# Value products in whole blocks of 128 queries, and an output projection of even units on 64x128 tiles

## The chip, the core and the metric

The kernel is one program on one core of a Trainium2 chip. Its engines work side by side, each in its own order, and wait for each other through semaphores: TensorE (PE in the profile, its weight loads PEld), VectorE (DVE), ScalarE (ACT), GpSimd (POOL) and SyncE (SP), which issues DMAs. The metric is the device time of one execution in microseconds (us). Lower is better.

## The reference

Attention over 8 batches and 8 heads of 576 positions with 64 dimensions, in which only scores within tau of their row's maximum count, then a mixture of 8 experts with one expert for each token:

```python
scores = scale * np.matmul(q, k.transpose(0, 1, 3, 2))
thresh = np.max(scores, axis=-1, keepdims=True) - tau
scores = np.where(scores >= thresh, scores, -1000000000.0)
attn = np.exp(scores - np.max(scores, axis=-1, keepdims=True))
x = np.matmul(attn / (np.sum(attn, axis=-1, keepdims=True) + 1e-09), v)   # tokens x 512, heads side by side
e_idx = np.argmax(x @ w_gate, axis=1)
...
out[mask] = gate_w[mask, None] * eom[mask, e, None] * (np.maximum(x[mask] @ w1[e], 0.0) @ w2[e])
```

All inputs and outputs are fp32.

## The kernel before

The attention treats a **unit** at a time: two batches (a = 0, 1) of one head, 32 units in all. The loop in `run` counts g through 16 **rounds** of nine **steps** (0 to 8). A round treats two units, an even one in steps 0 to 3 and an odd one in steps 5 to 8; step 4 (`ENDS`) takes the last 64 queries of both. In each step a string of letters (`USUAL`, `ROWS` and others) sets the order in which each engine receives its work; there is no scheduler.

- S, `scores` (L158 in step 4, L161 otherwise): 128 queries of both batches against 576 keys into PSUM. VectorE scales them and takes the row's extreme (L167), one instruction for each of two score tiles.
- e and f, `exp` (L177): ScalarE's exponentials of the two tiles. In the step after, VectorE masks and sums them (L189), with a threshold that GpSimd makes (L172).
- T, `remainder` (L222) and B, `blocks` (L264): TensorE transposes what was masked two steps earlier. o and c are ScalarE's copies of these out of PSUM: L247 (in step 4's turn four small ones, L237) and L279, into `PTa` (the first 256 queries) and `PTb` (the rest). L237's four copies take partitions 0-63, 64-127, 64-127, 0-63.
- V, `av_units` (L299): the value products. The weights are 64 columns of V for one batch and 128 keys (`vm[:, k, a]`, a 128x64 tile), or 64 keys at the end (64x64), and the transposed probabilities are read past them. An even unit's products stand in steps 5, 7 and 8 of its round, an odd unit's in steps 1, 2 and 3 of the next (`AV`). The sums stay in two PSUM banks (`self.banks`, named pab). X, `done`, copies them to SBUF (`X`, L303 and L305).
- R, `x_rows` (L341): the output projection. The stationary operand is a piece of `X`, 64 rows by 64 queries, the moving one `wx`: 80 columns, an identity of 64 and the 16 router weights. Even units have it in step 0, odd ones in step 4, between S and T. r, `x_copy` (L354), copies the result out of the same banks to `xl`; then GpSimd multiplies by the inverse sums (`x_out`, L363) and adds the logits.

In steps 0 and 4 the order is `ROWS = "SRTerofBc"`. On ScalarE this gives e, r, o, f, c. The value products of the following step write the banks that r and o read, and wait for o. R has its own place in PSUM at the very end alone.

In `X`, the 64-query block b of batch a lies on partitions of half a ^ (b % 2). Products of batch a and block parity o go to bank o and to half a ^ o. In steps other than 4, S, T and B use tiles of 64 rows by 128 columns, in step 4 S uses 64x64; R uses 64x64 in both places.

After the attention (about 450 us) the experts run on TensorE (L1184 to L1279) with the tokens that the router has sorted.

Of the kernel before, what the change touches and what calls it, by code (L numbers as in the profile page):

```python
# [8 lines left out]
F32 = mybir.dt.float32  # L9
# [7 lines left out]
P = 128  # L17
# [7 lines left out]
class Attention:  # L25
# [20 lines left out]
    def __init__(self, ctx, tc, ident, qkv, tau, wg, shape, router):  # L46
        self.tc, self.nc = tc, tc.nc
        nc = self.nc
        self.qkv = qkv
        self.B, self.H, self.S, self.D = shape  # L50
        self.NB = self.S // P
        self.M = self.NB * P
        self.R = self.S - self.M
        self.HS = self.S // 2
        self.KH = self.HS + self.R
        self.QK = 2 * self.S + 2 * self.KH
        self.QA = 2 * P
        self.NK = 2 * self.NB + 1
        self.nu = self.B // 2 * self.H
        self.router = router  # L60
        pool = lambda name, bufs, **kw: ctx.enter_context(tc.tile_pool(name=name, bufs=bufs, **kw))
        self.ld = pool("ald", self.LB)
        self.sp = pool("asp", 3)
        self.const = pool("aconst", 1)
        self.vld = pool("avld", self.VB)
        self.w2 = pool("aw2", 1)
        self.w3 = pool("aw3", 3)
        self.xp = pool("axp", 1)
        self.ps_s = pool("ps_s", 2, space=PSUM)
        self.ps_t = pool("ps_t", 1, space=PSUM)  # L70
        ab = pool("ps_ab", 1, space=PSUM)
        self.both = ab.tile([P, 1024], F32, name="pab").rearrange("p (a n) -> p a n", a=2)
        self.banks = [self.both[:, a] for a in range(2)]
        c = self.const
        self.ident = ident
        self.tau = c.tile([P, 1], F32, name="tau_sb")
        self.tau_in, self.wg_in = tau, wg
        warm = c.tile([P, 1], F32, name="warm")
        nc.vector.memset(warm, 0.0)
        nc.scalar.activation(warm, warm, AF.Exp)  # L80
        E2 = wg.shape[2]
        self.XW = self.D + E2
        self.wx = c.tile([P, self.H, self.XW], F32, name="wx")
        self.X = [c.tile([P, self.S], F32, name=f"X{i}") for i in range(2)]
        self.half = [slice(0, 64), slice(64, P)]
        for pp in self.half:
            nc.gpsimd.tensor_copy(
                self.wx[pp, :, 0 : self.D], ident[pp, None, pp].broadcast_to([self.D, self.H, self.D])
            )
        self.loaded, self.sums, self.rinv, self.LX = {}, {}, {}, None  # L90
        self.PTa, self.PTb, self.slot, self.live = {}, {}, 0, False
# [191 lines left out]
    def av_units(self, u):  # L283
        nc, NB, hs, D = self.nc, self.NB, self.half, self.D
        v = self.loaded[u][1]
        vm = v[:, 0 : NB * P].rearrange("p (k a d) -> p k a d", a=2, d=D)
        X = self.X[u % 2]

        def products(PT, half, k, start):
            PT = PT.rearrange("p k (b j) -> p k b j", j=D)  # L290
            nb, c0 = PT.shape[2], half * P
            for a, o in ((0, 0), (1, 0), (1, 1), (0, 1)) if k < NB else ((0, 0), (1, 1), (1, 0), (0, 1)):
                n = (nb - o + 1) // 2 * D
                out = self.banks[o][hs[a ^ o], c0 : c0 + n].rearrange("p (b j) -> p b j", j=D)
                if k < NB:
                    w, x, end = vm[:, k, a], PT[:, 4 * a + k, o::2], half and k == NB - 1
                else:
                    w, x, end = v[hs[a], NB * P :], PT[hs[a], self.NK - 1, o::2], not half
                nc.tensor.matmul(out, w, x, start=start, stop=bool(end), skip_group_check=True)  # L299

        def done(q0, c0, n):
            x = X[:, q0 : q0 + 2 * P].rearrange("p (b o j) -> p o b j", o=2, j=D)
            nc.scalar.copy(x, self.both[:, :, c0 : c0 + P].rearrange("p o (b j) -> p o b j", j=D))  # L303
            if n > 2 * P:
                nc.scalar.copy(X[:, q0 + 2 * P : q0 + n], self.banks[0][:, c0 + P : c0 + n - P])  # L305

        PT = self.PTa.pop(u)
        self.slot, self.live = 0, True
# [29 lines left out]

    def x_rows(self, u, ps):
        X, pp, W, h, NB = self.X[u % 2], self.half, self.XW, u % self.H, self.NB  # L340
        mm = lambda out, c0, k: self.nc.tensor.matmul(  # L341
            out, X[pp[k], c0 : c0 + 64], self.wx[pp[k], h], start=True, stop=True
        )
        for j in range(NB):
            for a in range(2):
                for c in range(2):
                    mm(ps[a][pp[c], j * W : (j + 1) * W], j * P + 64 * c, a ^ c)
        for a in range(2):
            mm(ps[0][pp[a], NB * W : (NB + 1) * W], self.M, a)

    def x_copy(self, xl, ps):
        for a, b in enumerate(ps):
            n = self.NB + 1 - a
            self.nc.scalar.copy(xl[:, a::2], b[:, 0 : n * self.XW].rearrange("p (j w) -> p j w", w=self.XW))  # L354

    def x_out(self, u, xl):
        nc, r, D, rt = self.nc, self.rinv[u], self.D, self.router
# [1143 lines left out]
```

## Time and profile before

| | |
|---|---|
| time, median of 3 runs | 874.05 us (871.35 to 875.64) |
| profiled execution | 871.86 us, its span 870.1 us |
| TensorE busy | 855.7 us, 98% of the span |
| VectorE busy | 716.7 us, 82% |
| ScalarE busy | 592.3 us, 68% |
| GpSimd busy | 442.6 us, 51% |
| granted TensorE clock, mean | 0.997 |

The shares are averages over two stages. In the slices of the page TensorE, VectorE and ScalarE stand at 9 tenths through the first half; in the second TensorE alone does. A busy TensorE is modelled: its rows overlap, and an end is later than the moment at which the next one can begin. Its pace is read from starts. A row of the timeline joins instructions that follow each other and are alike; every product in fp32 leaves two rows in the trace. A bracket gives the idle time ahead and what ended it.

### The profile page before, as it was taken

Reading aid. Unit: us, or ns where it says so; the run is one execution under the profiler, and the core shown is the slowest. Engines: PE = TensorE matmul, PEld = TensorE weight load, DVE = VectorE, ACT = ScalarE, POOL = GpSimd, SP = SyncE. Lnnn points to the kernel's source line nnn. Section 1 sums busy time; section 2 is a strip of 40 time slices with the busy share of each in tenths; the row PEclk is TensorE's granted clock in tenths of the full one; section 3 lists DMA queues with packets and bytes.
Section 4 is the critical chain, followed back from the end, with each engine's and each line's share of the span. In section 5 each row is a group of like instructions: output and inputs, shape, how many; then the busy total and the mean of one; then the engine's idle time right before and its main releaser. Section 6 shows DMA issues by size and latency. Waiting matters only on the chain. (4 is left out here: it accounts for less than half of the span.)

```text
span 870.1 us, 25698 instructions
## 1 busy us (share of the span) xinstructions
PE 855.7 (98%) x9993; PEld 720.7 (83%) x9993; DVE 716.7 (82%) x1788; ACT 592.3 (68%) x1130; POOL 442.6 (51%) x642
## 2 busy tenths in 40 slices
PE   8999999999999999999999999999999999999996
PEld 4777777777777777777779999999999988889885
DVE  7999999999999999999997768897677755558821
ACT  6999999999999999999985444444444524245611
POOL 4454544657746577556845446325563540434701
PEclk9999999999999999999999999999999999999998
DMA  5387763314433144323438668766888663549501
GB/s 166 115 282 258 261 205 115 118 60 153 137 114 117 60 142 146 118 78 111 146 76 239 232 171 220 205 170 198 227 241 216 202 178 104 158 131 253 169 13 49
DMA packets 89572, 138.20 MB, mean 159 GB/s; under 512 B 11493, under 2 KB 57447, under 8 KB 89448
## 3 DMA queue, kind: packets, MB, share of 16 engines
q1 hardware_dynamic: 81464, 115.37, 44.8%
q0 software_dynamic: 7984, 21.17, 6.5%
q8 instruction: 79, 1.29, 0.6%
q14 instruction: 45, 0.37, 0.1%
HBM read 104.43 MB, written 32.46 MB: 157 GB/s over the span
## 5 line engine op out<-in xcount | busy, mean ns | idle before, releaser
L177 ACT ACTIVATE p<-s,mn 128x576 f32<-128x576 f32 x288 | 213.7, 782 | 30.3 <-DVE s L167 29.6
L1298 POOL DMA_INDIRECT out_dram<-yo,idx x122 | 136.8, 1121 | 186.0 <-DVE yo L1292 150.6
L189 DVE SCALAR_TENSOR_TENSOR p<-s,thr,p 128x576 f32<-128x576 f32 x288 | 231.0, 838 | 0.6 <-POOL thr L172 0.6
L167 DVE TENSOR_SCALAR_CACHE_REDUCE s<-ps 128x576 f32<-128x576 f32 x288 | 204.9, 747 | 13.7 <-PE ps L158 8.0
L1189 ACT ACTIVATE hh<-ph 128x352 fp32r<-128x352 f32 (+4 forms) x96 | 47.2, 492 | 206.8 <-PE ph L1186 206.4
L172 POOL TENSOR_SCALAR thr<-mn,tau_sb 128x2 f32<-128x2 f32 x144 | 105.7, 734 | 157.5 <-DVE s L167 156.4
L161 PE MATMUL ps<-qk 64*128 64x288 f32 x1024 | 153.4, 418 | 0.4 <-DVE s L167 0.4
L1190 DVE SCALAR_TENSOR_TENSOR hl<-ph,hh 128x352 fp32r<-128x352 f32 (+4 forms) x96 | 53.4, 556 | 107.0 <-ACT hh L1189 106.4
L1184 PE MATMUL ph<-xh,w1h 128*128 128x352 f32 (+9 forms) x380 | 127.4, 335 | 1.1 <-ACT xl L354 1.1
L1185 PE MATMUL ph<-xl,w1h 128*128 128x340 f32 (+7 forms) x380 | 126.8, 334 | 0.2 <-DVE xl L978 0.2
L1186 PE MATMUL ph<-xh,w1l 128*128 128x340 f32 (+7 forms) x380 | 126.8, 334 | 0.0
L1277 PE MATMUL py<-hh,w2h 128*128 128x368 f32 (+8 forms) x320 | 106.7, 333 | 0.2 <-ACT hh L1189 0.2
L1278 PE MATMUL py<-hh,w2l 128*128 128x368 f32 (+5 forms) x320 | 106.2, 332 | 0.0
L1279 PE MATMUL py<-hl,w2h 128*128 128x340 f32 (+5 forms) x316 | 105.1, 333 | 0.0
L161 PEld LDWEIGHTS ps<-qk 64*128 64x128 f32 x1024 | 86.7, 189 | 17.9 <-DVE s L167 5.7
L299 PE MATMUL pab<-PTb,vld 128*64 128x128 f32 (+3 forms) x1280 | 97.4, 304 | 0.0
L264 PE MATMUL pt<-ident,p 64*128 64x64 f32 x2288 | 95.9, 223 | 0.0
L299 PEld LDWEIGHTS pab<-PTb,vld 128*64 128x64 f32 (+1 forms) x1280 | 71.8, 136 | 25.7 <-issue 9.1
L264 PEld LDWEIGHTS pt<-ident,p 64*128 64x128 f32 x2288 | 83.2, 139 | 1.8 <-issue 0.2
L299 PEld LDWEIGHTS pab<-PTa,vld 128*64 128x64 f32 (+1 forms) x1280 | 61.9, 136 | 25.9 <-ACT PTb L247 12.4
L299 PE MATMUL pab<-PTa,vld 128*64 128x128 f32 (+1 forms) x1280 | 77.5, 280 | 0.5 <-ACT PTb L247 0.2
L1184 PEld LDWEIGHTS ph<-xh,w1h 128*128 128x128 f32 x380 | 71.4, 188 | 5.1 <-ACT xl L354 1.3
(249 smaller groups left out, 1535.3 us busy)
## 6 DMA issues: line engine op xcount, KB each, us to landing
r<-in_moe_w_dram SPq DMA_DIRECT2D x104, 512.0 KB
qk<-in_qkv_dram SPq DMA_DIRECT2D x31, 928.0 KB
vld<-in_qkv_dram SPq DMA_DIRECT2D x32, 288.0 KB
xs<-zrow SPq DMA_DIRECT2D x24, 357.5 KB
xg<-xs SPq DMA_DIRECT2D x24, 178.8 KB
xg<-xs SPq DMA_DIRECT2D x12, 260.0 KB
xs<-zrow SPq DMA_DIRECT2D x8, 260.0 KB
out_dram<-yo,idx POOLq DMA_INDIRECT x122
```

The source lines that it names most:

```text
L161: nc.tensor.matmul(ps[x][:, cs], q, k, start=True, stop=True)
L167: nc.vector.tensor_scalar(s, ps[a][:, c0 : c0 + S], SC, None, op0=ALU.mult, op1=ALU.min, accum_out=mn[:, a : a + 1])
L177: self.nc.scalar.activation(e, ss[a], AF.Exp, bias=mn[:, a : a + 1], scale=-1.0)
L189: nc.vector.scalar_tensor_tensor(e, s, thr[:, a : a + 1], e, op0=ALU.is_le, op1=ALU.mult, accum_out=sums[a])
L264: nc.tensor.transpose(pt[:, o : o + 64], p[hs[h], k0 : k0 + P], id_[hs[h], hs[h]])
L299: nc.tensor.matmul(out, w, x, start=start, stop=bool(end), skip_group_check=True)
L1184: nc.tensor.matmul(ph[:, 0:n], w1h[:, c, fs], self.xh[:, c, 0:n], start=(c == 0), stop=False)
L1185: nc.tensor.matmul(ph[:, 0:N], w1h[:, c, fs], self.xl[:, c, 0:N], start=False, stop=False)
L1186: nc.tensor.matmul(ph[:, 0:N], w1l[:, c, fs], self.xh[:, c, 0:N], start=False, stop=(c == 3))
L1277: nc.tensor.matmul(y[:, 0:n], wh[:, c], hh[:, 0:n], start=(f == 0), stop=False)
L1278: nc.tensor.matmul(y[:, 0:N], wl[:, c], hh[:, 0:N], start=False, stop=False)
L1298: ins = nc.gpsimd.indirect_dma_start(out=out, out_offset=bass.IndirectOffsetOnAxis(ap=self.idx[:, b : b + 1], axis=0), in_=yo[:, b - b0], ...
```

## The change

Three things change.

- Value products: parity o no longer picks every second block of 64 queries but a whole block: the first 128 queries of a half for o = 0, the rest (128 or 192) for o = 1. What is read is contiguous. With it the layout of `X` changes: a block of 128 queries of batch a lies on half a ^ (block % 2). `done` copies without splitting into blocks of 64, and takes the last 64 queries from the other bank.
- The projection of an even unit multiplies pieces of 128 queries, 64x128 tiles, row half r into bank r: ten products where there were eighteen. Its last 64 queries are covered by a piece that reaches past the end of X for r = 1 (X is 64 columns wider, and GpSimd sets these to zero at the start) and by one that begins 64 queries earlier for r = 0. An odd unit keeps 64x64 tiles and eighteen products, in another order.
- `x_copy` makes four copies where there were two: each bank's four blocks of 128 queries (320 columns), and then the last 64 queries, 80 columns from each bank on one half of the partitions.

```diff
@@ -81,7 +81,9 @@
         E2 = wg.shape[2]
         self.XW = self.D + E2
         self.wx = c.tile([P, self.H, self.XW], F32, name="wx")
-        self.X = [c.tile([P, self.S], F32, name=f"X{i}") for i in range(2)]
+        self.X = [c.tile([P, self.M + P], F32, name=f"X{i}") for i in range(2)]
+        for x in self.X:
+            nc.gpsimd.memset(x[:, self.S :], 0.0)
         self.half = [slice(0, 64), slice(64, P)]
         for pp in self.half:
             nc.gpsimd.tensor_copy(
@@ -287,22 +289,21 @@
         X = self.X[u % 2]
 
         def products(PT, half, k, start):
-            PT = PT.rearrange("p k (b j) -> p k b j", j=D)
-            nb, c0 = PT.shape[2], half * P
+            c0 = half * P
             for a, o in ((0, 0), (1, 0), (1, 1), (0, 1)) if k < NB else ((0, 0), (1, 1), (1, 0), (0, 1)):
-                n = (nb - o + 1) // 2 * D
-                out = self.banks[o][hs[a ^ o], c0 : c0 + n].rearrange("p (b j) -> p b j", j=D)
+                q = slice(P, PT.shape[2]) if o else slice(0, P)
+                out = self.banks[o][hs[a ^ o], c0 : c0 + q.stop - q.start]
                 if k < NB:
-                    w, x, end = vm[:, k, a], PT[:, 4 * a + k, o::2], half and k == NB - 1
+                    w, x, end = vm[:, k, a], PT[:, 4 * a + k, q], half and k == NB - 1
                 else:
-                    w, x, end = v[hs[a], NB * P :], PT[hs[a], self.NK - 1, o::2], not half
+                    w, x, end = v[hs[a], NB * P :], PT[hs[a], self.NK - 1, q], not half
                 nc.tensor.matmul(out, w, x, start=start, stop=bool(end), skip_group_check=True)
 
         def done(q0, c0, n):
-            x = X[:, q0 : q0 + 2 * P].rearrange("p (b o j) -> p o b j", o=2, j=D)
-            nc.scalar.copy(x, self.both[:, :, c0 : c0 + P].rearrange("p o (b j) -> p o b j", j=D))
+            x = X[:, q0 : q0 + 2 * P].rearrange("p (o j) -> p o j", o=2)
+            nc.scalar.copy(x, self.both[:, :, c0 : c0 + P])
             if n > 2 * P:
-                nc.scalar.copy(X[:, q0 + 2 * P : q0 + n], self.banks[0][:, c0 + P : c0 + n - P])
+                nc.scalar.copy(X[:, q0 + 2 * P : q0 + n], self.banks[1][:, c0 + P : c0 + n - P])
 
         PT = self.PTa.pop(u)
         self.slot, self.live = 0, True
@@ -338,20 +339,27 @@
 
     def x_rows(self, u, ps):
         X, pp, W, h, NB = self.X[u % 2], self.half, self.XW, u % self.H, self.NB
-        mm = lambda out, c0, k: self.nc.tensor.matmul(
-            out, X[pp[k], c0 : c0 + 64], self.wx[pp[k], h], start=True, stop=True
-        )
-        for j in range(NB):
-            for a in range(2):
-                for c in range(2):
-                    mm(ps[a][pp[c], j * W : (j + 1) * W], j * P + 64 * c, a ^ c)
+        for j in range(NB + 1):
+            for r in range(2):
+                cs = slice(j * W, j * W + W)
+                if u % 2 == 0:
+                    c0 = j * P if j < NB or r else j * P - 64
+                    parts = [(ps[r][:, cs], c0, P)]
+                else:
+                    halves = range(2) if j < NB else (1 - r,)
+                    parts = [(ps[r][pp[c], cs], j * P + 64 * c * (j < NB), 64) for c in halves]
+                for out, c0, n in parts:
+                    self.nc.tensor.matmul(out, X[pp[r], c0 : c0 + n], self.wx[pp[r], h], start=True, stop=True)
+
+    def x_copy(self, xl, ps):
+        nc, W, NB, pp = self.nc, self.XW, self.NB, self.half
+        x = xl[:, 0 : 2 * NB].rearrange("p (m o) w -> p m o w", o=4)
+        for r, b in enumerate(ps):
+            nc.scalar.copy(
+                x[:, :, 1:3] if r else x[:, :, 0::3], b[:, 0 : NB * W].rearrange("p (m o w) -> p m o w", o=2, w=W)
+            )
         for a in range(2):
-            mm(ps[0][pp[a], NB * W : (NB + 1) * W], self.M, a)
-
-    def x_copy(self, xl, ps):
-        for a, b in enumerate(ps):
-            n = self.NB + 1 - a
-            self.nc.scalar.copy(xl[:, a::2], b[:, 0 : n * self.XW].rearrange("p (j w) -> p j w", w=self.XW))
+            nc.scalar.copy(xl[pp[a], 2 * NB], ps[1 - a][pp[a], NB * W : (NB + 1) * W])
 
     def x_out(self, u, xl):
         nc, r, D, rt = self.nc, self.rinv[u], self.D, self.router
```

How TensorE's order stands at step 0 (x_rows of an even unit, L341; wx is the moving operand, X the stationary one). Before:

```order
L264 MATMUL pt<-ident,p 128x64 x16
L161 MATMUL ps<-qk 128x288 x4
L341 MATMUL pab<-wx,X_227 64x80 x18
L222 MATMUL pab<-ident,p 128x64 x2
L264 MATMUL pt<-ident,p 128x64 x16
L161 MATMUL ps<-qk 128x288 x4
L299 MATMUL pab<-PTa,vld 64x128 x16
```

and in the changed kernel:

```order
L266 MATMUL pt<-ident,p 128x64 x16
L163 MATMUL ps<-qk 128x288 x4
L352 MATMUL pab<-wx,X_227 128x80 x10
L224 MATMUL pab<-ident,p 128x64 x2
L266 MATMUL pt<-ident,p 128x64 x16
L163 MATMUL ps<-qk 128x288 x4
L300 MATMUL pab<-PTa,vld 64x128 x16
```

Nothing has moved; eighteen products into 64 partitions have become ten into 128.

ScalarE's order around x_copy (L354, later L358 and L362) in steps 0 and 4, with the semaphores that it waits for. Before:

```order
L279 COPY PTa<-pt 128x8x128 [waits PE_49]
L177 ACTIVATE p<-s,mn 128x576 [waits DVE_49]
L354 COPY xl<-pab 128x5x80 [waits PE_49,Activation_49,Pool_49]
L354 COPY xl<-pab 128x4x80
L247 COPY PTb<-pab 128x128
L177 ACTIVATE p<-s,mn 128x576 [waits DVE_49]
```

and in the changed kernel:

```order
L281 COPY PTa<-pt 128x8x128 [waits PE_49]
L179 ACTIVATE p<-s,mn 128x576 [waits DVE_49]
L358 COPY xl<-pab 128x2x2x80 [waits PE_49,Activation_49,Pool_49]
L358 COPY xl<-pab 128x2x160
L362 COPY xl<-pab 64x80 x2
L249 COPY PTb<-pab 128x128
L179 ACTIVATE p<-s,mn 128x576 [waits DVE_49]
```

Two copies of 64 partitions stand between the large ones and the remainder's copy (L247, later L249).

## Rows read from the trace of the kernel before

**Rows 1.** Groups by line and shape, VectorE, 20 to 450 us: busy, mean | idle before

```profile
L167 DVE TENSOR_SCALAR_CACHE_REDUCE s<-ps 128x576 f32<-128x576 f32 x276 | 196.4, 747 | 9.6 <-PE ps L158 8.0 <-PE ps L161 0.4
```

**Rows 2.** Timeline, TensorE, round 8, steps 0 and 1: start, busy us, instruction [idle before]

```profile
222.02 1.19 PE L161 MATMUL ps<-qk 64*128 64x288 f32 x8
223.14 0.91 PE L341 MATMUL pab<-wx,X 64*64 64x80 f32 x36
223.98 0.28 PE L222 MATMUL pab<-ident,p 64*128 64x64 f32 x2
...
224.04 0.58 PEld L264 LDWEIGHTS pt<-ident,p 64*128 64x128 f32 x16
224.53 0.79 PEld L161 LDWEIGHTS ps<-qk 64*128 64x128 f32 x8
225.71 0.31 PEld L299 LDWEIGHTS pab<-PTa,vld 128*64 128x64 f32 x6 [0.38 <-ACT PTb L247]
```

**Rows 3.** Timeline, TensorE, round 7, steps 4 and 5

```profile
207.41 1.20 PE L158 MATMUL ps<-qk 64*64 64x288 f32 x16
...
209.23 0.28 PE L222 MATMUL pab<-ident,p 64*128 64x64 f32 x2
...
210.96 1.97 PE L299 MATMUL pab<-PTa,vld 128*64 128x128 f32 x32
```

**Rows 4.** Timeline, ScalarE, round 7 step 4, then round 8 step 0

```profile
208.99 0.78 ACT L177 ACTIVATE p<-s,mn 128x576 f32<-128x576 f32 x1 [0.40 <-DVE s L167]
...
209.67 0.80 ACT L354 COPY xl<-pab 128x400 f32<-128x400 f32 x2
...
223.60 0.78 ACT L177 ACTIVATE p<-s,mn 128x576 f32<-128x576 f32 x1
224.38 0.82 ACT L354 COPY xl<-pab 128x400 f32<-128x400 f32 x2
225.08 0.28 ACT L247 COPY PTb<-pab 128x128 f32<-128x128 f32 x1
```

**Rows 5.** Timeline, ScalarE's copy and TensorE's weight load behind it, rounds 5 and 7

```profile
142.33 0.28 ACT L247 COPY PTb<-pab 128x128 f32<-128x128 f32 x1
...
142.76 0.20 PEld L299 LDWEIGHTS pab<-PTa,vld 128*64 128x64 f32 x4 [0.39 <-ACT PTb L247]
...
197.70 0.28 ACT L247 COPY PTb<-pab 128x128 f32<-128x128 f32 x1
...
198.17 0.31 PEld L299 LDWEIGHTS pab<-PTa,vld 128*64 128x64 f32 x6 [0.39 <-ACT PTb L247]
```

**Rows 6.** Timeline, ScalarE in step 6, TensorE's weight load in step 7, round 7

```profile
215.03 0.78 ACT L177 ACTIVATE p<-s,mn 128x576 f32<-128x576 f32 x1 [0.33 <-DVE s L167]
215.71 0.19 ACT L237 COPY PTb<-pab 64x64 f32<-64x64 f32 x1
...
215.91 0.21 ACT L237 COPY PTb<-pab 64x64 f32<-64x64 f32 x1
...
216.02 0.21 ACT L237 COPY PTb<-pab 64x64 f32<-64x64 f32 x1
...
216.24 0.20 ACT L237 COPY PTb<-pab 64x64 f32<-64x64 f32 x1
216.35 0.58 ACT L273 COPY PTb<-pt 128x512 f32<-128x512 f32 x1
...
216.50 0.21 PEld L299 LDWEIGHTS pab<-PTa,vld 64*64 64x64 f32 x8 [0.47 <-ACT PTb L237]
```

**Rows 7.** Timeline, GpSimd at the start: a copy on partitions 64-127, the first threshold

```profile
6.37 0.61 POOL L87 COPY wx<-ident 64x512 f32<-64x512 f32 x1
7.08 0.32 POOL L172 TENSOR_SCALAR thr<-mn,tau_sb 128x2 f32<-128x2 f32 x1
```

**Rows 8.** Timeline, TensorE's weight loads of the first experts, end of the attention

```profile
451.06 0.19 PEld L1184 LDWEIGHTS ph<-xh,w1h 128*128 128x128 f32 x1 [1.32 <-ACT xl L354]
...
467.30 0.19 PEld L1277 LDWEIGHTS py<-hh,w2h 128*128 128x128 f32 x1 [0.34 <-ACT hh L1189]
```

## The prediction

> **What bounds the kernel now.** I read the page's slices first (which engine is full in which stretch), then VectorE's groups by line, then the timelines of a few steps, engine by engine. The kernel has two stages. Up to about 450 us the attention runs in 16 rounds of nine steps (0 to 8), two units a round; after it the experts keep TensorE full, and what they do is not touched. So only the attention can move. There the lines view shows what VectorE does between its rows: over 430 us it idles 9.6 us ahead of the score reductions, and 8.0 of these end with the scores of L158, which are those of step 4 [rows 1]. VectorE is therefore the engine that never rests, and once a round, at step 4, it stands still because TensorE is late. From 9.6 us, whatever TensorE gains cannot save more.
>
> Why is TensorE late just there? Steps 1, 2 and 3 each hold value products, and step 6 holds none. Follow one round: at step 6 ScalarE's first exponential waits 0.33 us for VectorE, and the value products of step 7 start 216.50, 0.05 us after the last L237 copy ended (216.24 + 0.20) [rows 6]. So at step 7 TensorE is held by ScalarE. From there to step 4 of the next round it works without a pause longer than a change of tile size, and each of its delays on that way is paid by VectorE at step 4. A microsecond taken from TensorE between step 7 and step 4 is a microsecond of the round, if nothing else holds TensorE on the way.
>
> One thing nearly does. The value products of step 1 write the banks that x_copy and the remainder's copy (L247) read in step 0, and wait for that L247. In round 8 L247 ends 225.08 + 0.28 = 225.36 and the products' first weight load starts 225.71: a margin of 0.35 us [rows 2, 4]. In round 5 it is 142.76 - 142.61 = 0.15, in round 7 198.17 - 197.98 = 0.19 [rows 5]. The 0.05 us of step 7 is what a held start looks like, so 0.30, 0.10 and 0.14 are to spare. Seven rounds (1 to 4, 8, 12, 15) look like round 8, three (5, 9, 13) like round 5, two (7, 11) like round 7; 6, 10 and 14 lie between rounds 7 and 8 and are taken halfway, 0.27, or 0.22 to spare.
>
> **Value products: nothing.** Number, tiles and column sums of the products are the same; 192 columns move from one bank to the other. If the 64-column pieces cost reading time, products in pieces would be slower per column than the scores, which read in one piece. 32 rows of 128 columns, two at a time, are busy 1.97 us (0.96 ns a column); 8 rows of 288 columns, two at a time, 1.19 us (1.03 ns) [rows 2, 3]. They are not. The copies of done() keep their elements.
>
> **Projection of an even unit (step 0): 0.28 us of TensorE.** Its 64x64 tiles stand between 64x128 ones, so the tile size changes ahead of it and behind it. From the first score row to the remainder's first row step 0 takes 223.98 - 222.02 = 1.96 us, step 4 209.23 - 207.41 = 1.82 [rows 2, 3]. Both hold four turns of scores and the same 36 projection rows; step 0 holds two changes of size, step 4 one. A change costs 0.14 us. The change removes two: 0.28. The rows themselves: 16 products of two rows go four at a time, the last two two at a time, ten turns, in 223.98 - 223.14 - 0.14 = 0.70 us, or 0.07 a turn. Afterwards 20 rows go two at a time: ten turns again. A turn now loads 128 weight columns; the transposes do that eight times from 224.04 to 224.53, 0.061 us each [rows 2], less than the 0.07 that the 80 columns take. So 0.70 stays, and 0.28 is gained.
> The Trainium skill (TensorE: Matmul & The Clock Gate, section LDWEIGHTS) puts a weight load at columns over 1.2, 107 ns for 128. By that estimate the ten turns would take 1.07 us, TensorE would lose 0.09 us a round, and the sum below would be +3.2 instead of +2.4; the 0.061 us of the transposes speaks against it, and what is left of it lies in the chance of rival D.
>
> **Projection of an odd unit (step 4): nothing.** Eighteen products in another order; four that follow each other still use four different tiles, in the order in which L158 uses them.
>
> **x_copy: 0.38 us more of ScalarE, in every unit.** Before, two copies (400 and 320 columns) take 225.08 - 224.38 = 0.70 us to the next start [rows 4]. After, two of 320 take 0.70 less at most 80/720 of it, about 0.64. Then come two copies of 80 columns, on partitions 0-63 and on 64-127. Nearest are L237's four of 64 columns, whose halves go first, second, second, first: starts 215.71, 215.91, 216.02, 216.24, then the next copy at 216.35 [rows 6]. Where the half stays, or a first half is followed by all 128 partitions, the next starts after 0.11; where the half changes it starts only after the record has ended, 0.20 and 0.22. So the first small copy takes 0.21 + 0.01 for its 16 columns more. For the second, a second half followed by all partitions, ScalarE shows no row: 0.12 if it overlaps, 0.22 if not. I take 0.22, since GpSimd's copy of a second half ended 6.98 and the next began 7.08 [rows 7], without overlap. Sum 1.08: **+0.38**; +0.28 with the other end, +0.18 if neither small copy waits.
> The Trainium skill (ScalarE: Activation LUTs, section What ACT_TABLE_LOAD costs) lets neighbouring activations overlap by about 93 ns, which makes 160 ns of each small copy and +0.26; 215.91 shows no overlap where the half changes, 216.02 shows it where it stays.
>
> **What of this meets.** At step 0 x_copy stands ahead of L247. It waits for the remainder's transposes: in round 8 it starts 0.77 us after the exponential before it, at step 4, unheld, 0.68 [rows 4]. With TensorE 0.28 earlier that 0.10 comes back (in rounds like 8 alone). So L247 ends 0.28 later in those and 0.38 later in the others, and step 1's value products move by that less what was to spare: -0.30 + 0.28 = -0.02 (seven rounds), -0.10 + 0.38 = +0.28 (three), -0.14 + 0.38 = +0.24 (two), -0.22 + 0.38 = +0.16 (three). Sum -0.14 + 0.84 + 0.48 + 0.48 = **+1.7 us**. TensorE's 0.28 is lost: it arrives early at products that ScalarE holds. With +0.28 a copy the sum is +0.2, with +0.18 it is -1.3.
> At step 4 the same 0.38 lies on ScalarE, which idles 0.33 ahead of step 6's exponential [rows 6]; the rest, 0.05 in 15 rounds, is 0.75 at most, and I count nothing. GpSimd's multiplication by the inverses waits for the last copy and is not awaited before the round ends.
> At the end of the attention the cover is gone: the first expert product waits 1.32 us for x_copy, and at 467.30 an expert product waits 0.34 us for ScalarE, which is held there by the routing that begins with the last x_copy [rows 8]. Each is 0.38 later: **+0.4 to +0.8**, I take 0.76, since both stand on the way of TensorE.
> The two memsets of X stand in GpSimd's start, ahead of the first threshold at 7.08 [rows 7]. I count nothing; if nothing covered them, a few tenths, once.
>
> Sum: 1.7 + 0.76 = +2.4 us. On the profiled execution's 871.86 that is 874.3; the median of three runs stands 2.2 above it, at 874.05, and gives **876.4**.
>
> **Rivals.**
> A, the small copies overlap: +0.28 or +0.18 a copy, drain 0.56 or 0.36: +0.7 or -1.0, 873.0 to 874.8. For it: 0.11 us where the half stays. Against it: 0.20 and 0.22 where it changes.
> B, x_copy costs ScalarE nothing: then step 1 moves by what was to spare, at most 0.28: 7 x 0.28 + 0.30 + 0.28 + 0.66 = 3.2 us saved, 870.9. Against it stand two more instructions on an engine that runs in order.
> C, slower, ScalarE runs out: a small copy costs as much as one of 320 columns (0.32), because a half is written alone. x_copy +0.58: step 1 moves by +0.18, +0.48, +0.44, +0.36, together 4.7; drain 1.16: +5.8, 879.9. It decides from about +0.5 a copy, beyond the 0.33 us of step 6. Against it: no L237 row is longer than 0.21.
> D, the wide tile's weight loads are not hidden: turns of 0.061 + 0.07 = 0.13, projection 1.3 us, TensorE +0.32 a round and no longer waiting for ScalarE: 15 x 0.32 + 0.76 = +5.6, 879.6. That the tile change stays would matter less: with TensorE's gain at zero only seven rounds move, by 0.02.
>
> **Chances.** Forecast 0.48, A 0.26, B 0.09, C 0.12, D 0.05. A difference of 0.5%, 4.4 us, is about what a measurement of this kernel can tell from none. Forecast, A and B lie inside; C and D outside, and the forecast's own tail adds a little: faster 0.04, same 0.78, slower 0.18. The three runs before differ by 4.3 us. The range goes from B, less what runs differ, to C: 870.0 to 880.0.
>
> **What the changed profile would show.** Step 0: the projection's 20 rows take 0.70 us, with no pause ahead of or behind them; a row time of 0.84 would refute the 0.28, one of 1.3 is D. ScalarE: about 1.08 us from the first copy of x_copy to L247's successor; 0.88 is A. Step 1: value products start 0.05 us after that copy ended, in every round. Step 4: VectorE idles longer than before in rounds like 5 and 7, as long in rounds like 8. If step 4's idle time falls in all rounds, ScalarE did not hold step 1 and the forecast is wrong by its sign.

## The result: 0.67% slower, and the profile after

The changed kernel takes 878.89 us (median of 6 runs, 877.58 to 879.24), the kernel before 872.73 (6 runs, 871.35 to 875.64): a ratio of 1.0067, 95% interval 1.0051 to 1.0082. That is +6.2 us where +2.4 was forecast; the time lies inside the range of 870 to 880, but it is "slower by over 0.5%", which had a chance of 0.18, and not "within 0.5%", which had 0.78. The profiled execution of after has a span of 877.5 us, 7.4 longer than before.

Line numbers move by the change: the score reduction L167 is now L169, the scores L158 and L161 are L160 and L163, the remainder's transposes L222 are L224 and its copies L237 and L247 are L239 and L249, the blocks L264 are L266 and their copy L279 is L281, the projection L341 is L352, and x_copy is L358 (the copies of 320 columns) and L362 (the small ones).

**Where the time is lost.** VectorE's group of score reductions from 20 to 458 us (busy, mean | idle before) answers to [rows 1]:

```profile
L169 DVE TENSOR_SCALAR_CACHE_REDUCE s<-ps 128x576 f32<-128x576 f32 x277 | 197.4, 749 | 14.3 <-PE ps L160 9.5 <-PE ps L163 2.4
```

It idles 14.3 us instead of 9.6, because TensorE is late. A round is measured from the first score reduction of one step 4 to that of the next; here in rounds 7 and 8, in VectorE's timeline (start, busy us, instruction [idle before]), of before and then of after:

```profile
208.19 0.76 DVE L167 TENSOR_SCALAR_CACHE_REDUCE s<-ps 128x576 f32<-128x576 f32 x1 [0.71 <-PE ps L158]
...
235.74 0.76 DVE L167 TENSOR_SCALAR_CACHE_REDUCE s<-ps 128x576 f32<-128x576 f32 x1 [0.71 <-PE ps L158]
```

```profile
211.96 0.76 DVE L169 TENSOR_SCALAR_CACHE_REDUCE s<-ps 128x576 f32<-128x576 f32 x1 [0.71 <-PE ps L160]
...
239.96 0.76 DVE L169 TENSOR_SCALAR_CACHE_REDUCE s<-ps 128x576 f32<-128x576 f32 x1 [0.71 <-PE ps L160]
```

A round takes 28.00 us instead of 27.55, and the same 0.4 to 0.5 is lost in nearly every round. Over the 15 periods from round 0 to round 15 it is 421.01 - 414.59 = 6.42 us. Nearly all the rest of the 7.4 between the two spans is no loss of the change: 0.94 stands ahead of step 4 of round 0, and three experiments below with the same start (the same two memsets; a_narrow, a_swap and a_co2) lose only 0.2 there; from the last score reduction to the end of the span before needs 427.8 and after 427.7. That last stretch is a poor measure: in the traces of b_three, b_split_odd, b_split_even and b_ot the granted clock falls to 0.5 (1.2 GHz) for 3.4 or 6.8 us at the end of the attention, from 451 to 455 us on, where TensorE waits, and the stretch takes 429.8 to 431.8 us; the costs below go by the 15 periods, which lie ahead of it.

At step 4 VectorE waits 0.71 us in rounds 7 and 8 in both kernels, and 0.65 instead of 0.38 in round 5: longer in rounds like 5 and as long in round 8, as the prediction said, but not longer in round 7, where it said so too. The rest of the loss reaches VectorE in other steps: in round 8 it waits 0.32 instead of 0.12 at step 2 and 0.12 instead of nothing at step 6.

**Step 0.** TensorE's timeline of round 8, to be read beside [rows 2]:

```profile
226.05 1.19 PE L163 MATMUL ps<-qk 64*128 64x288 f32 x8
227.07 1.24 PE L352 MATMUL pab<-wx,X 64*128 64x80 f32 x20
228.15 0.22 PE L224 MATMUL pab<-ident,p 64*128 64x64 f32 x2
```

The two pauses are gone, as the prediction said: the projection starts right behind the scores and the transposes right behind the projection. But its ten turns take 228.15 - 227.07 = 1.08 us, 0.11 each, not 0.07. From the first score row to the first transpose TensorE now needs 2.10 us instead of 1.96: it loses 0.14 a round where it was to win 0.28.

**x_copy.** ScalarE's timeline, step 4 of round 7 and step 0 of round 8, beside [rows 4]; and TensorE's first value product of step 1 behind it:

```profile
213.44 0.73 ACT L358 COPY xl<-pab 128x320 f32<-128x320 f32 x2
214.07 0.45 ACT L362 COPY xl<-pab 64x80 f32<-64x80 f32 x2
214.54 0.27 ACT L249 COPY PTb<-pab 128x128 f32<-128x128 f32 x1
...
227.61 0.78 ACT L179 ACTIVATE p<-s,mn 128x576 f32<-128x576 f32 x1
228.49 0.75 ACT L358 COPY xl<-pab 128x320 f32<-128x320 f32 x2
229.13 0.46 ACT L362 COPY xl<-pab 64x80 f32<-64x80 f32 x2
229.61 0.27 ACT L249 COPY PTb<-pab 128x128 f32<-128x128 f32 x1
```

```profile
229.92 0.41 PEld L300 LDWEIGHTS pab<-PTa,vld 128*64 128x64 f32 x7 [0.48 <-ACT PTb L249]
```

x_copy takes 1.10 us at step 4 and 1.12 at step 0, against 0.70 before (forecast 1.08). The value products of step 1 start 0.04 after L249's end (229.61 + 0.27): ScalarE holds them, as forecast.

**What the prediction did not look at.** ScalarE in steps 5 and 6 of round 7, then TensorE's weight loads of step 6's blocks and step 7's value products. First before, in rows that [rows 6] lack, then after:

```profile
213.43 0.27 ACT L247 COPY PTb<-pab 128x128 f32<-128x128 f32 x1
213.68 1.02 ACT L279 COPY PTb<-pt 128x1024 f32<-128x1024 f32 x1
```

```profile
214.26 0.38 PEld L222 LDWEIGHTS pab<-ident,p 64*128 64x128 f32 x4
214.75 0.58 PEld L264 LDWEIGHTS pt<-ident,p 64*128 64x128 f32 x16
```

```profile
217.62 0.26 ACT L249 COPY PTb<-pab 128x128 f32<-128x128 f32 x1
217.77 1.03 ACT L281 COPY PTb<-pt 128x1024 f32<-128x1024 f32 x1
218.93 0.78 ACT L179 ACTIVATE p<-s,mn 128x576 f32<-128x576 f32 x1
...
218.85 0.58 PEld L266 LDWEIGHTS pt<-ident,p 64*128 64x128 f32 x16 [0.30 <-ACT PTb L281]
...
220.52 0.21 PEld L300 LDWEIGHTS pab<-PTa,vld 64*64 64x64 f32 x8 [0.38 <-ACT PTb L239]
```

The blocks of step 6 start 0.05 after the copy of step 5's blocks has ended, in after (217.77 + 1.03 = 218.80) and already in before (213.68 + 1.02 = 214.70): both use the one pair of banks that the copy empties. So TensorE had no time to spare against ScalarE there; in before its row shows no idle time only because the four loads of the remainder (214.26) stand in the wait. ScalarE's 0.33 us of idle time lie behind that copy, ahead of the exponential, and do not help.

### The profile page after: what moved, and what is told of

Its sections match the earlier page's. It is cut to its first block, busy times and chain, and to the rows that moved or that the text cites. A ratio compares the mean times of both kernels' runs of the same rounds, so it can differ in the third digit from the quotient of the medians.

```text
span 877.5 us, 25252 instructions
## 1 busy us (share of the span) xinstructions
PE 859.9 (98%) x9737; PEld 724.6 (83%) x9737; DVE 717.6 (82%) x1788; ACT 603.8 (69%) x1194; POOL 444.3 (51%) x644
## 5 line engine op out<-in xcount | busy, mean ns | idle before, releaser
L169 DVE TENSOR_SCALAR_CACHE_REDUCE s<-ps 128x576 f32<-128x576 f32 x288 | 205.3, 749 | 19.2 <-PE ps L160 9.5
L163 PE MATMUL ps<-qk 64*128 64x288 f32 x1024 | 154.3, 420 | 0.0
L1193 PE MATMUL ph<-xl,w1h 128*128 128x340 f32 (+7 forms) x380 | 126.6, 333 | 0.0
L163 PEld LDWEIGHTS ps<-qk 64*128 64x128 f32 x1024 | 88.7, 190 | 16.5 <-DVE s L169 2.6
L266 PE MATMUL pt<-ident,p 64*128 64x64 f32 x2288 | 95.9, 223 | 2.5 <-ACT PTb L281 2.5
L300 PE MATMUL pab<-PTb,vld 128*64 128x192 f32 (+3 forms) x1280 | 97.6, 304 | 0.0
L266 PEld LDWEIGHTS pt<-ident,p 64*128 64x128 f32 x2288 | 83.1, 139 | 4.9 <-ACT PTb L281 4.6
L300 PEld LDWEIGHTS pab<-PTb,vld 128*64 128x64 f32 (+1 forms) x1280 | 67.4, 136 | 23.5 <-issue 14.7
```

The source lines that it names most:

```text
L163: nc.tensor.matmul(ps[x][:, cs], q, k, start=True, stop=True)
L169: nc.vector.tensor_scalar(s, ps[a][:, c0 : c0 + S], SC, None, op0=ALU.mult, op1=ALU.min, accum_out=mn[:, a : a + 1])
L266: nc.tensor.transpose(pt[:, o : o + 64], p[hs[h], k0 : k0 + P], id_[hs[h], hs[h]])
L1193: nc.tensor.matmul(ph[:, 0:N], w1h[:, c, fs], self.xl[:, c, 0:N], start=False, stop=False)
```

## The experiments

For each kernel the table has the period from step 4 to step 4 into rounds 2, 5 and 6 (three of the kinds of rounds), and the sum of all 15 periods of its trace, worked out from the starts of the score reductions; the last column is the difference of that sum to before.

```
kernel          into 2   into 5   into 6   15 periods   to before
before           27.55    27.65    27.86     414.59
b_three          27.55    27.64    27.86     414.68       +0.09
b_split_odd      27.79    27.79    27.96     417.20       +2.61
b_split_even     27.64    27.94    28.04     417.37       +2.78
b_split_all      27.89    28.08    28.07     419.35       +4.76
a_narrow         27.91    28.09    28.09     419.60       +5.01
after            27.99    28.15    28.26     421.01       +6.42
a_swap           27.99    28.16    28.25     421.03       +6.44
a_co2            27.95    28.16    28.25     420.81       +6.22
b_ot             27.47    27.63    27.86     413.94       -0.65
```

The second table follows one round (2) through TensorE: the start of the first row of each place, counted from the score reduction of step 4, in before, and how much later it is in the others.

```
                        before   odd    even   all    a_narrow  after   b_ot
value products, step 5   2.77   +0.13   0.00  +0.13   +0.14    +0.14   0.00
blocks, step 6           6.56   +0.32   0.00  +0.33   +0.33    +0.34   0.00
value products, step 7   8.31   +0.25   0.00  +0.25   +0.25    +0.25  -0.08
scores, step 0          13.83   +0.25   0.00  +0.25   +0.26    +0.26  -0.08
remainder, step 0       15.79   +0.25   0.00  +0.25   +0.27    +0.40  -0.08
value products, step 1  17.52   +0.25  +0.10  +0.35   +0.36    +0.45  -0.08
reduction, step 4       27.55   +0.25  +0.09  +0.35   +0.37    +0.45  -0.08
```

**x_copy by itself, in all units, in odd ones, in even ones.** The kernel before, with only the changed kernel's four copies (n is the 4 blocks, m too where the copy is split, and split holds for all, odd or even units):

```
-            n = self.NB + 1 - a
-            self.nc.scalar.copy(xl[:, a::2], b[:, 0 : n * self.XW].rearrange("p (j w) -> p j w", w=self.XW))
+            self.nc.scalar.copy(xl[:, a : a + 2 * m - 1 : 2], b[:, 0 : m * W].rearrange("p (j w) -> p j w", w=W))
+        for pp in self.half if split else ():
+            self.nc.scalar.copy(xl[pp, 2 * n], ps[0][pp, n * W : (n + 1) * W])
```

> The kernel before with the changed kernel's x_copy alone: two copies of 320 columns, then the last 80 columns as two copies of 64 partitions, for every unit. x_copy should take 1.12 us to the next start instead of 0.70, +0.42 on ScalarE. Theory P (the prediction's): step 4's share is absorbed in the idle time of step 6; step 0's, less what was to spare (0.30 in seven rounds, 0.10 in three, 0.14 in two, 0.22 in three), moves step 1: 0.84 + 0.96 + 0.56 + 0.60 = 3.0, and 0.7 at the end of the attention: +3.7 on 872.7, 876.4. Theory Q (read from the changed kernel's trace): step 4's share also reaches TensorE, through the copy of step 5's blocks that frees the bank pair for step 6's blocks, and makes step 7's value products 0.25 late in every round; step 1 then moves by the larger of the two: 1.75 + 0.96 + 0.56 + 0.75 = 4.0, with 0.7 at the end +4.7, 877.4. If the two add, +7.5, 880.2.

> The same split of x_copy in odd units alone, whose x_copy runs in step 4; even units keep the two copies of before. Theory P: absorbed in ScalarE's idle time of step 6, +0 to +0.75, 872.7 to 873.5 (up to 0.4 more at the end of the attention). Theory Q: TensorE's blocks of step 6 wait for the copy of step 5's blocks, 0.25 a round, 15 rounds: +3.8, 876.5; in the trace the period from step 4 to step 4 grows by 0.25 and the first block of step 6 starts 0.05 after the end of that copy with 0.1 to 0.2 us of waiting.

> The same split in even units alone, whose x_copy runs in step 0. Both theories: step 1's value products start 0.05 after the remainder's copy in every round and move by +0.42 less what was to spare, 3.0 us in 15 rounds, and 0.3 at the end of the attention: +3.3, 876.0. A rival, in which ScalarE's lateness at step 0 is no limit because TensorE is later anyway: under +0.5, 873.2.

Measured: in all units 876.65 us (before in the same runs 872.43; ratio 1.0040, 1.0026 to 1.0054), in odd units 874.84 (1.0018, 1.0007 to 1.0028), in even units 875.46 (1.0030, 1.0018 to 1.0043). By the trace the odd units cost 2.61 us in 15 rounds, where theory P had at most 0.75 and theory Q 3.8. In the trace of the odd split ScalarE's copy of step 5's blocks ends at 216.36, and the blocks of step 6 start 0.04 later, with the wait on it:

```profile
215.33 1.03 ACT L279 COPY PTb<-pt 128x1024 f32<-128x1024 f32 x1
...
216.40 0.57 PEld L264 LDWEIGHTS pt<-ident,p 64*128 64x128 f32 x16 [0.30 <-ACT PTb L279]
```

So theory P falls, and Q's path is there; Q's 0.25 holds in rounds like 2 and is 0.14 and 0.10 in rounds 5 and 6. In round 5 the 0.25 is there at the scores of step 0, but the projection behind them is only 0.16 late; in round 6 the blocks of step 6 are 0.32 late and the value products of step 7 only 0.11, since these start 0.12 later than in round 2 already in before (8.43 against 8.31). The even units cost 2.78, near the 3.0 that both theories had: at step 0 the working of the prediction was right, 0.10 in rounds like 2 (0.42 less the 0.30 to spare), 0.29 in rounds like 5. One round (8) lost 0.38 there, because its x_copy began 0.27 late; why is open. That step 1 moves by the larger of the two, as Q had it, is wrong: 0.25 and 0.10 make 0.35, 0.14 and 0.29 make 0.43. TensorE's lateness reaches VectorE at step 0's scores and with it ScalarE's exponential, so x_copy starts late already: in b_split_all by 0.26 in round 2, 0.14 in round 5 and 0.01 in round 6. Only in rounds like 6 (0.10 + 0.18, measured 0.21) is the sum smaller.

**The narrow projection in the changed kernel.** All units use 64x64 tiles:

```
-                if u % 2 == 0:
+                if False:
                     c0 = j * P if j < NB or r else j * P - 64
```

> The changed kernel with the projection of even units on 64x64 tiles like that of odd units; value products, layout of X and the four copies of x_copy stay as in the changed kernel. The projection of step 0 goes back to 0.70 us with a pause of 0.14 ahead of it and behind it, instead of 1.12 without. If whole-block value products cost nothing (theory P and Q), it takes as long as the kernel before with the split of x_copy in all units, by Q 877.4, and the wide tiles cost the rest, 1.5 us, since the remainder's transposes come 0.14 earlier than in the changed kernel. Rival: the value products cost something, then it takes longer than that kernel, up to 878.9.

Measured: 876.88 us (1.0053, 1.0034 to 1.0073), beside 876.65 for the split in all units. The trace agrees to 0.25 us in 15 rounds: that is all that value products on whole blocks cost, together with done's copies and the new order of the narrow projection, which differ as well. The changed kernel's 421.01 less 419.60 leaves **1.41 us for the wide tiles**. TensorE's rows of step 0 of round 8 in this kernel:

```profile
224.71 1.19 PE L163 MATMUL ps<-qk 64*128 64x288 f32 x8
225.82 0.92 PE L352 MATMUL pab<-wx,X 64*64 64x80 f32 x36
226.67 0.28 PE L224 MATMUL pab<-ident,p 64*128 64x64 f32 x2
```

From the first score row to the first projection row it is 1.11 us here and 1.02 in the changed kernel, from there to the first transpose 0.85 (with the pause behind it) and 1.08. The wide tiles win 0.09 ahead and lose 0.23 after, and the remainder comes 0.14 later: the +0.40 against +0.27 of the second table.

**Why a turn takes 0.11: the weight loads.** The changed kernel with its blocks (L266) turned by plain products with the identity in place of transposes, with the same tiles and the same 128 weight columns and 64 streamed ones:

```
-                nc.tensor.transpose(pt[:, o : o + 64], p[hs[h], k0 : k0 + P], id_[hs[h], hs[h]])
+                nc.tensor.matmul(pt[:, o : o + 64], p[hs[h], k0 : k0 + P], id_[hs[h], hs[h]], start=True, stop=True)
```

> The changed kernel with the blocks of the attention weights turned by plain products with the identity instead of by transposes: same tiles, same 128 weight columns, same 64 columns streamed, 16 rows a step, two at a time. It measures the disputed cost by itself. If a load of 128 weight columns for a plain product takes 0.11 us and nothing hides it (the 0.1115 us per turn of the changed kernel's wide projection), the eight turns take 0.11 instead of 0.061 each, 0.4 us more in each of 144 steps, and since TensorE and VectorE are close to even, up to 50 us more: 900 to 930. Rival: the load is no slower than that of the transposes and the 0.11 comes from writing 128 partitions of two banks by 80 columns: the turns stay 0.06 to 0.07, 879.

Measured: 1053.1 us. The weight loads of the blocks in the two traces, by line (busy, mean ns), first after and then this kernel, and the timeline's row of one step of the latter:

```profile
L266 PEld LDWEIGHTS pt<-ident,p 64*128 64x128 f32 x2288 | 83.1, 139 | 4.9 <-ACT PTb L281 4.6 <-issue 0.3
```

```profile
L266 PEld LDWEIGHTS pt<-ident,p 64*128 64x128 f32 x4576 | 272.5, 191 | 2.2 <-ACT p L179 0.3 <-ACT PTa L281 0.2
```

```profile
299.32 1.42 PEld L266 LDWEIGHTS pt<-ident,p 64*128 64x128 f32 x23
```

The load of a transpose is recorded with 139 ns, that of a product of the same shape with 191; 23 loads, two at a time, start within 1.42 - 0.19 = 1.23 us, 0.112 a turn, where transposes take 0.061. The products write the same 128 partitions of the same banks as the transposes, so the rival falls. The turn is as long with 64 columns streamed here as with 80 in the wide projection (0.108), so it does not follow the stream; that the load sets it is inferred from this and from the records. The transposes' 0.061 need not be a load either: 64 columns at the pace of the scores (four turns of 288 columns in 223.14 - 222.02 = 1.12 us [rows 2], 0.97 ns a column) take 0.062, so their load is only known to take no longer. The expectation's total was wrong since I had not counted that a plain fp32 product takes two rows on TensorE and a transpose one (4576 rows against 2288): 16 turns of 0.112 less 8 of 0.061 are 1.30 us a step, 187 us in 144 steps; 174 were measured.

**The order of the small copies.**

```
-        for a in range(2):
+        for a in (1, 0):
             nc.scalar.copy(xl[pp[a], 2 * NB], ps[1 - a][pp[a], NB * W : (NB + 1) * W])
```

> The changed kernel with the two small copies of x_copy in the other order: partitions 64-127 first, then 0-63. In the changed kernel the first takes 0.235 to the next start and the second 0.245, since the half changes after the one and all 128 partitions follow an upper half after the other. If it is the change of start partition that keeps two copies of ScalarE from overlapping, a lower half followed by all 128 partitions overlaps (0.11, as at the last copy of the remainder in step 6), x_copy takes 1.0 us instead of 1.12, and the 0.12 come back at both places: about 0.1 to 0.2 a round, 1.5 to 3 us, 876 to 877.4. Rival: a copy of half the partitions costs 0.24 wherever it stands: no change, 878.9.

Measured: 878.69 us (1.0064, 1.0047 to 1.0082), 421.03 in the trace: no change. ScalarE's rows of step 4:

```profile
212.68 0.73 ACT L358 COPY xl<-pab 128x320 f32<-128x320 f32 x2
213.43 0.45 ACT L362 COPY xl<-pab 64x80 f32<-64x80 f32 x2
213.79 0.26 ACT L249 COPY PTb<-pab 128x128 f32<-128x128 f32 x1
```

The small copies do take less, 213.79 - 213.43 = 0.36 instead of 0.47, but the large ones ahead of them take 0.75 instead of 0.63: the upper half now waits for the end of the copy on all partitions. Both orders change the start partition twice, and each change costs 0.11 to 0.13. My expectation had counted only the change behind.

**The same 80 columns in one piece.** The kernel before with three copies, the third on all 128 partitions:

```
+        self.nc.scalar.copy(xl[:, 2 * n], ps[0][:, n * W : (n + 1) * W])
```

> The kernel before with x_copy in three copies for every unit: 320, 320 and then the last 80 columns on all 128 partitions. One instruction more than before, one less than in the kernel with the split in halves, and every start at partition 0. If it is the change of the start partition that costs, the third copy overlaps its neighbours, x_copy takes about 0.76 us instead of 0.70 (1.12 with the halves), and the round grows by 0.01 to 0.06: 0.2 to 0.9 us, 873.0 on 872.5. Rival: a further instruction on ScalarE costs 0.24 however many partitions it has: x_copy 0.88 to 0.94, about half of the 4.2 us of the split, 874.6.

Measured: 872.63 us (before in these runs 872.09; 1.0007, 0.9996 to 1.0018), +0.09 us in the trace. ScalarE's rows of step 4:

```profile
210.31 0.73 ACT L354 COPY xl<-pab 128x320 f32<-128x320 f32 x2
210.93 0.24 ACT L355 COPY xl<-pab 128x80 f32<-128x80 f32 x1
211.05 0.29 ACT L247 COPY PTb<-pab 128x128 f32<-128x128 f32 x1
```

x_copy takes 211.05 - 210.31 = 0.74. A third copy of 80 columns costs 0.12 to the next start, and all of the 4.76 us of the split but 0.09 come from its halves; 0.09 is less than the 0.2 to 0.9 expected. The rival (0.24 for any instruction more) falls.

**Step 6's blocks earlier in the changed kernel.**

```
-    ORDER = {6: "SeToBcf"}
+    ORDER = {5: "SefVTBcoX", 6: "SeBTocf"}
```

> The changed kernel with two orders changed: in step 5 ScalarE copies the blocks ahead of the remainder, and in step 6 TensorE turns the blocks ahead of the remainder. Nothing is taken away; only the copy that frees the bank pair for step 6's blocks comes some 0.15 earlier on ScalarE. If step 4's x_copy costs time through this copy (theory Q), step 6's blocks start earlier, step 7's value products come 0.1 earlier in each round, limited by ScalarE's copies of step 6, which VectorE holds: about -1.5 us, 877.4. Rival: the blocks are not on the path, and the lateness of step 7 comes from step 5's value products alone, 0.13 late: no change, 878.9.

Measured: 878.20 us (1.0057, 1.0039 to 1.0075), which this measurement can't tell from after; -0.2 us in the trace. TensorE's rows of step 6, and scores and value products of step 7:

```profile
217.83 0.72 PE L266 MATMUL pt<-ident,p 64*128 64x64 f32 x16
218.38 0.29 PE L224 MATMUL pab<-ident,p 64*128 64x64 f32 x4
218.51 1.19 PE L163 MATMUL ps<-qk 64*128 64x288 f32 x8
219.63 0.45 PE L300 MATMUL pab<-PTa,vld 64*64 64x128 f32 x8
```

In rounds like 2 the blocks start 0.17 earlier, but the remainder, which had filled TensorE's wait, now stands behind them and takes 218.51 - 218.38 = 0.13. What is left, 0.04, arrives whole: step 7's value products and the period are both 0.04 earlier. The path is the one of theory Q; the gain expected was too large by the cost of the remainder.

**ScalarE's hold of step 7 taken away in the kernel before.**

```
-    ORDER = {6: "SeToBcf"}
+    ORDER = {6: "SToeBcf"}
```

> The kernel before with one order changed: in step 6 ScalarE's four copies of the remainder go ahead of the first exponential instead of behind it, into the 0.33 us in which it idles. Step 7's value products then no longer wait for these copies and start when TensorE is free, 0.1 earlier; a microsecond saved for TensorE there should be one of the round until ScalarE's copy of step 0 holds step 1, 0.30 to 0.10 further: about -0.1 a round, -1.5 us on 872.4, 870.9. Rival: the exponential, 0.3 to 0.4 later, and the copies behind it hold the products of step 8 or VectorE instead: no gain, or slower by up to 0.3 a round, 877.

Measured: 873.04 us (before in the same runs 872.62; 0.9998, 0.9985 to 1.0011): no difference that can be measured. The trace has -0.08 in rounds like 2 and nothing to -0.02 in rounds like 5 and 6, -0.65 in all. So step 7's value products were held by ScalarE's four copies, as the prediction read it, but by 0.08 only. That is also why the 0.33 of step 6 is 0.25 at step 7.

## Why the prediction was right or wrong

**What bounds the kernel: right.** VectorE waits at step 4 for TensorE, and what TensorE loses between step 7 and step 4 is lost by the round: each of the second table's columns keeps its value from step 1 to the reduction of step 4. (In rounds like 5, 0.09 of it comes back at the projection of step 0.)

**Value products: right.** 0.25 us in 15 rounds, other small differences included (a_narrow against b_split_all).

**x_copy's size: right.** 1.10 to 1.12 us against the 1.08 forecast; the choice of 0.22 for the second small copy, for which ScalarE had shown no row, was right (it takes 0.24). a_swap and b_three show the cause that the prediction gave, the change of the start partition.

**x_copy at step 0: right.** The spare times of 0.30 to 0.10 hold: b_split_even loses 2.78 us, and the same working with the measured 0.42 gives 3.0. Only the 0.10 that the prediction took off in seven rounds, for an earlier TensorE, did not come, since the projection ends later and not earlier.

**x_copy at step 4, "the rest, 0.05 in 15 rounds, is 0.75 at most, and I count nothing": wrong.** This is the largest miss, 2.6 us (b_split_odd). The prediction held the whole of ScalarE's lateness against its 0.33 us of idle time at step 6. But an engine's idle time helps only what stands behind it in its queue. Ahead of it stands the copy of step 5's blocks, and TensorE was already waiting for that copy in before: 213.68 + 1.02 = 214.70, blocks at 214.75. Of the 0.42, 0.10 came back ahead of this copy (it starts 0.25 after L247 in before, 217.77 - 217.62 = 0.15 after L249 in after), 0.32 reached the blocks of step 6, and 0.08 was idle time of TensorE at step 7: 0.25 a round in rounds like 2. There the prediction's sentence that TensorE works without a pause from step 7 on was right, and it tells why nothing gave these 0.25 back; in rounds 5 and 6 all but 0.14 and 0.10 did come back.

**Projection of even units: wrong by its sign.** The pauses went, as forecast, but the term "0.061, less than the 0.07 that the 80 columns take. So 0.70 stays" failed: the turns take 0.11 and the projection 1.08 us. The 0.061 was read from transposes, and a_plain shows that turns of products with the same 128 weight columns take 0.11. TensorE loses 0.14 instead of winning 0.28, and the wide tiles cost 1.41 us (a_narrow). This is the mechanism of rival D, which had a chance of 0.05; D's price of 0.13 a turn was wrong: the turn is no longer with 80 columns streamed than with 64, so load and stream do not add.
The Trainium skill (TensorE: Matmul & The Clock Gate, section LDWEIGHTS) gives columns over 1.2, 107 ns for 128, and the prediction worked out 1.07 us from it. The trace of after agrees: 1.08. For transposes it does not hold, with turns of 0.061. The rule was set aside for a row of another kind of instruction.

**The end of the attention, +0.76: wrong.** TensorE's weight loads, to be read beside [rows 8]; first the one behind the 451.06 of before, then after's:

```profile
451.71 0.19 PEld L1185 LDWEIGHTS ph<-xl,w1h 128*128 128x128 f32 x1 [0.46 <-DVE xl L978]
```

```profile
458.83 0.19 PEld L1192 LDWEIGHTS ph<-xh,w1h 128*128 128x128 f32 x1 [1.64 <-ACT xl L362]
458.94 0.19 PEld L1193 LDWEIGHTS ph<-xl,w1h 128*128 128x128 f32 x1
...
474.55 0.19 PEld L1285 LDWEIGHTS py<-hh,w2h 128*128 128x128 f32 x1 [0.27 <-ACT hh L1197]
```

The first expert product waits 0.32 longer, near the 0.38 forecast, but the second wait did not grow (0.27 against 0.34), and it comes 15.72 us after the first one instead of 16.24. What gave the 0.3 back stands in the row between. In before the next load (L1185) waits another 0.46 for VectorE, whose transposes of the tokens had waited for a DMA; in after it (L1193) follows 0.11 behind the first. VectorE's rows, before and then after:

```profile
447.80 1.96 DVE L1166 STREAM_TRANSPOSE s<-xg 128x384 f32<-128x384 f32 x4 [1.75 <-DMA xg<-xs]
```

```profile
453.46 1.95 DVE L1174 STREAM_TRANSPOSE s<-xg 128x384 f32<-128x384 f32 x4
```

The five kernels whose last score reduction starts by 445.2 us (before, b_three, b_split_odd, b_split_even, b_ot) all wait for this DMA, 1.75 to 3.2 us; the five that reach it between 447.2 and 449.9 us (b_split_all, a_narrow, a_swap, a_co2 and after) do not. By these ten traces it is the later end of the attention that took the wait away, and so it hides a part of what the change loses. No run shows the second 0.38.

**The sum.** Forecast: 1.7 in the rounds and 0.76 behind them. Measured in the traces: 2.61 for step 4's copies, 2.15 for step 0's on top of them, 0.25 for the value products, 1.41 for the wide projection, together 6.42, and about nothing behind them in the one trace of each. The medians differ by 6.2. That the time still lies inside the range is in part luck: the 874.05 from which 876.4 was worked out stands 1.3 above the median of six runs, 872.73, and the range is 10 us wide. From 872.73 the forecast would have been 875.1, and what was missed is 3.8 us. VectorE's idle time ahead of its reductions explains 4.7 of it; in what form the other 1.7 appears on VectorE was not followed.

**The rivals.** A and B fell with x_copy's size. C had the right total (+5.8) for the wrong reason: no small copy costs as much as a large one, and the rest of ScalarE's lateness came by step 5's copy, which no case of the prediction names.

## What to carry to other kernels

Before a delay is set against an engine's idle time, look which instruction that idle time stands ahead of, and whether another engine waits for one that stands earlier in the queue: a start 0.05 us behind the end of a copy was a hold here, with nothing to spare, even where the row's idle time looks like that of a change of tiles. A price for an instruction is to be read from one of the same kind; a transpose's turn is no bound for a product's. Wider tiles saved two changes of tile size here and lengthened every turn, whose weight load was then longer than its stream: two pauses, 0.28 us together by the prediction's estimate, against ten turns that are 0.04 longer.

## What the runs showed of the hardware

- Fp32 products with 128 weight columns by 64 rows, two at a time, take 0.11 us a turn, with 80 columns streamed (after, 0.108) as with 64 (a_plain, 0.112): the stream is hidden, by all signs behind the weight load. Transposes of the same shape take 0.061, about what their 64 columns take to stream, so their load takes no longer than that.
- Two of these copies of ScalarE out of PSUM overlap by about 0.1 us if they start at the same partition, and not at all if one starts at partition 0 and the next at 64 or the other way round (after, a_swap). It is the start that counts and not the number of partitions: a copy on partitions 0 to 63 overlaps with one on all 128. Eighty columns cost 0.12 us to the next start in one piece (b_three), and 0.47 in two halves (after).
- A plain fp32 product takes two rows on TensorE, a transpose one (4576 against 2288).
